# The states in three groups, batch 0's x packed by two engines, and a retimed slot table

## The chip, the core and the metric

The kernel runs on one core of a Trainium2 chip. Time is the device time of one execution in microseconds (us), a median over runs. A profile is one execution, taken by the hardware profiler; its span runs from the first to the last instruction of the program.

## What is computed

Cross attention between tokens x and a small state, both ways, and then a feed-forward layer with a snake activation on the concatenated result:

```python
# x: (8, 8, 512, 64), state: (8, 8, 32, 64); B, H, S, D = x.shape, Ns = 32
scores = scale * np.matmul(x, state.transpose(0, 1, 3, 2))
a = softmax(scores)
xread = np.matmul(a, state)                     # 512 tokens a batch
scores2 = scale * np.matmul(state, x.transpose(0, 1, 3, 2))
sread = np.matmul(softmax(scores2), x)          # 32 tokens a batch
t = np.concatenate([xread, sread], axis=2)      # 8 batches of 544 tokens, 512 wide
h = t @ w_in                                    # 512 x 2048
s = np.sin(alpha * h)
out = (h + s * s / alpha) @ w_out               # 2048 x 512
```

## The kernel before

**Tiles and slots.** The feed-forward part runs over nine tiles t: tiles 0 to 7 are the 512 read tokens of one batch each, tile 8 the 256 state tokens of all batches. A tile has 16 slots f, one for each 128 of the 2048 hidden columns. The order of each engine's instructions is that of the Python program (a manual schedule), and each engine works off its own queue in order.

In a slot, `mm1` makes a 128 x 512 block of h in a bank of the pool `psH` (four banks) on TensorE, two matmuls; ScalarE takes its sine (line 405); the square goes to VectorE (DVE, line 417) where the slot is listed in the table `SQ`, else to GpSimd (POOL, line 410); and two slots later DVE's `snake` (line 420) makes gT = s2/alpha + h and frees the bank. A tile's second product, `mm2` (line 429), is 64 matmuls of 216 ns each for four blocks of 128 tokens; the tables `TWO0`, `TWO1` and `TWO` say how many of them follow in each slot of tile 0, 1 and the later ones. When a block is done ScalarE copies it out (line 435) and SP stores it.

**Attention.** mm1 for tiles 0 to 7 does not multiply xread by w_in: `m_step` first makes M = state times w_in for each batch (16 or 8 groups of small matmuls a call, line 373, four slices `fs` of 512 columns, two halves g each), cast out of PSUM by ScalarE (line 383) or DVE (line 385) as the table 'MA' says; mm1 then multiplies M by the transposed attention weights AT. For one batch the steps are: load x (POOL, cast to bf16), `pack` (DVE), transposed x (`T` by TensorE in batches 0 and 1, `T_dma` by a transposing DMA from SP later), `S` (scores), `X` (exp on ScalarE, with a load of the table of functions before and after), `Rs` (sums, DVE), `N` (product A, on POOL, or on DVE where `ND` lists it), AT (`AT_` or `AT_dma`), and for the state tokens `W`, `Cs` and `xs`.

`BATCH` gives for each of these steps the slot, counted from the start of the batch's preceding tile (M and W: from its own tile), at which it is put into the program; batches from 3 on share the last entry. `pe` steps come after the mm1 of their slot, `post` steps at the slot's end.

**The front.** Before tile 0 the program loads all states (512 KB) and batch 0's x on SP. A copy `held` on POOL waits for the states, so that the loads of w_in ("i"), w_out ("o") and x ("x") that POOL issues behind it, in the order of `LOADS`, don't compete with them; the first `LATER` of them come at once, the others after batch 0's first product A. `prep_state` doubles all states (DVE and ScalarE), transposes them on TensorE in 16 pieces and copies them to `stT` (ScalarE, line 218). `warm_up(n)` issues n matmuls without a use. The pool `psX` (tag "px") has two banks, shared by T, S, AT_, W and the M step; `psO` has two, for mm2 and the M step.

Of the kernel before, what the change touches and what calls it, by code (L numbers as in the profile page):

```python
# [12 lines left out]
BF16 = mybir.dt.bfloat16  # L13
FP32 = mybir.dt.float32
U32 = mybir.dt.uint32
# [7 lines left out]
BATCH = {0: {'M': (-24, 1, 6, 7), 'MA': ((1, 0), (1, 1), (1, 1), (1, 1))},  # L23
 1: {'P': (1, 1),
# [4 lines left out]
     'N': (11, 9),  # L29
     'A': 14,  # L30
     'M': (-6, 1, 3, 10),
     'MA': ((1, 1), (1, 1), (1, 1), (1, 1)),
     'W': (5, 5)},
 2: {'L': -16,
     'P': (1, 3),
     'T': 5,
     'S': (6, 6),
     'X': (6, 6),
     'R': (6, 9),
     'N': (8, 10),  # L40
     'A': 12,
     'M': (-3, 1, 5, 7),
     'MA': ((0, 1), (1, 1), (1, 1), (1, 1)),
     'W': (-1, 0)},
 3: {'L': -17,
     'P': (-13, -11),
     'T': -8,
     'S': (0, 2),
     'X': (2, 2),
     'R': (5, 8),  # L50
     'N': (9, 12),
     'A': 14,
     'M': (-4, -3, 4, 4),
     'MA': ((0, 1), (1, 1), (0, 1), (1, 0)),
     'W': (-2, -2)}}

SQ = {0: (0, 1, 2, 4, 5, 8, 9, 11, 14, 15),
 1: (1, 2, 3, 5, 6, 7, 8, 11, 14),
 2: (3, 5, 6, 13, 15),
 7: (0, 1, 2, 4, 7, 8, 12),  # L60
 8: (0, 5, 7, 8, 12, 14)}
ND = {1: (), 2: (), 3: (1,)}

SLICES = {0: ((0,), (1,), (2,), (3,)), 1: ((0,), (1,), (2,), (3,)), 2: ((0, 1), (2, 3)), 3: ((0, 1), (2, 3))}
XS0 = 0

TWO0 = (0, 0, 0, 1, 2, 0, 2, 0, 2, 0, 0, 6, 1, 1, 6, 1)
TWO1 = (2, 3, 5, 1, 3, 0, 5, 2, 3, 2, 3, 5, 1, 6, 1, 0)
TWO = (1, 2, 6, 3, 10, 5, 3, 3, 4, 3, 5, 0, 5, 4, 4, 6)
WARM = (7, 1, 2, 2, 0, 1, 2)  # L70
LATER = 6

LOADS = ('i0', 'i1', 'x1', 'o0', 'i2', 'i3', 'o1', 'o2', 'o3')
# [3 lines left out]
def kernel(  # L77
# [9 lines left out]
    nc = tc.nc  # L87

    B, H, S, D = x.shape
    Ns = state.shape[2]  # L90
# [36 lines left out]
    st_nat = const.tile([P, 16, D], FP32, name="st_nat")  # L127
    nc.sync.dma_start(
        st_nat[:], state.rearrange("b h (jh jl) d -> (b h jh) jl d", jl=16)
    )  # L130
# [25 lines left out]
    nc.gpsimd.tensor_copy(held[:], st_nat[:, 0, 0:1])  # L156
# [5 lines left out]
    def load(what, k):  # L162
        k = int(k)
        if what == "x":
            load_x(k, 1)
        elif what == "i":
            cols = slice(k * FW, (k + 1) * FW)
            nc.gpsimd.dma_start(w_in_sb[:, :, cols], w_in_v[:, :, cols])  # L168
        else:
            fts = slice(k * 4, (k + 1) * 4)  # L170
            nc.gpsimd.dma_start(w_out_sb[:, fts, :], w_out_v[:, fts, :])

    for w in LOADS[:LATER]:
        load(*w)
# [7 lines left out]
    stT = const.tile([P, B * G, P], BF16, name="stT")  # L182
    nc.vector.memset(stT[:].bitcast(U32), 0)
# [15 lines left out]
    def prep_state():  # L199
        st2 = const.tile([P, 16, 2, D], BF16, name="st2")  # L200
        for half, copy in ((0, nc.vector.tensor_copy), (1, nc.scalar.copy)):
            js = slice(half * 8, (half + 1) * 8)
            copy(st2[:, js], st_nat[:, js].unsqueeze(2).to_broadcast([P, 8, 2, D]))
        for half in range(2):
            tp = psH.tile([P, 8, P], BF16, name="st_ps", tag="h")
            for k in range(8):
                nc.tensor.transpose(
                    tp[:, k, :],
                    st2[:, half * 8 + k].rearrange("p r d -> p (r d)"),
                    ident[:],  # L210
                )
            for r in range(2):
                rows = slice(r * D, (r + 1) * D)
                src = tp[rows].rearrange("d k (e r2 jh) -> d e r2 jh k", r2=2, jh=2)
                dst = stT[rows].rearrange(
                    "d bg (h2 r2 jh hf k) -> d (bg h2) r2 jh hf k", h2=2, r2=2, jh=2, hf=2
                )
                nc.scalar.copy(dst[:, :, r, :, half, :], src[:, :, r])
# [7 lines left out]
    class Att:  # L226
# [13 lines left out]
        def pack(a, g, parts=2):  # L240
            hs = slice(g * H // parts, (g + 1) * H // parts)
            nc.vector.tensor_copy(  # L242
                a.xp[:, :, hs, :],
                xnat_l[a.b][:, hs, :].rearrange("p h (i d) -> p i h d", i=C),
            )

# [27 lines left out]
        def S(a, g):  # L274
            sp = psX.tile([P, C, P], FP32, name="s_ps", tag="px")
            for i in range(C):
                for k in range(2):
                    cols = slice(k * 2 * Ns, (k + 1) * 2 * Ns)
                    nc.tensor.matmul(  # L279
                        sp[:, i, cols],  # L280
                        a.xT[:, i, 2 * g + k, :],
                        stT[:, a.b * G + g, cols],
                        start=True, stop=True,
                    )
            a.sp[g] = sp
# [71 lines left out]
    def m_step(b, slices, on_act):  # L357
# [8 lines left out]
        for fs in slices:  # L366
            for h in range(2):
                for g in range(G):
                    for r in range(2):
# [5 lines left out]
                            stT[rows, b * G + g, c0:c0 + Ns],  # L375
# [93 lines left out]
    prep_state()  # L469
# [4 lines left out]
    a.pack(0)  # L474
    a.pack(1)
# [28 lines left out]
    def add(d, s, fn, *args):  # L504
        d.setdefault(s, []).append((fn, args))
# [7 lines left out]

    for b in range(B):
        p = BATCH[min(b, 3)]
# [3 lines left out]
        if b:  # L519
# [10 lines left out]
            for g in range(G):  # L530
# [3 lines left out]
                eng = nc.vector if g in ND[min(b, 3)] else nc.gpsimd  # L534
# [80 lines left out]
```

## Time and profile before

| | us |
|---|---|
| median of 5 runs (lowest, highest) | 231.41 (230.69, 231.78) |
| the profiled execution | 230.69 |
| its span | 228.9 |
| busy: TensorE (PE), DVE, ScalarE (ACT), POOL | 212.5, 170.8, 164.6, 111.5 |
| states land, x of batch 0 lands (two halves) | 4.68; 6.19 and 7.58 |
| w_in slices land | 11.1, 13.6, 22.5, 25.1 |
| x of batches 1, 2 and 3 lands | 16.4, 35.4, 38.7 |
| first mm1; first sine of tiles 1 and 2 | 13.96; 34.2, 55.9 |

Times in the lower rows are counted from the start of the span. PE is TensorE's matmuls, PEld its weight loads, which lie beside them. Matmul ends are modelled, so a hole on TensorE is read from the starts: one start to the next, less the usual pitch of that form.

### The profile page before, as it was taken

How to read it: one execution, taken by the hardware profiler on the slowest of the kernel's cores; microseconds unless marked ns; L12 is line 12 of the kernel's file. 1: busy time of each engine (PE TensorE's matmuls, PEld its weight loads, DVE VectorE, ACT ScalarE, POOL GpSimd, SP SyncE). 2: the span in 40 equal slices, each digit the busy share in tenths (PEclk: the TensorE clock that was granted, in tenths of full speed). 3: DMA queues.
4: the chain of work that ended last, by engine and by line, in shares of the span. 5: the costliest groups of instructions: out<-in, count | busy, mean ns of one | idle time of the engine just before them, and what ended most of it. 6: DMA issues, size and time to landing. Idle time of an engine off the chain costs nothing.

```text
span 228.9 us, 4186 instructions
## 1 busy us (share of the span) xinstructions
PE 212.5 (93%) x1508; PEld 103.5 (45%) x1536; DVE 170.8 (75%) x309; ACT 164.6 (72%) x266; POOL 111.5 (49%) x120
## 2 busy tenths in 40 slices
PE   6987799799989999999999999999997999999993
PEld 2634243444434544454444444454443444556552
DVE  3699999998498969795988788877876796544500
ACT  4689979988996699667967796769783766444420
POOL 3871581265629651975168625843481135632210
PEclk9999999999999999999999999999999999999998
DMA  6999999823716381659063805220208101111112
GB/s 210 194 196 206 206 186 168 179 72 92 92 49 139 95 136 46 139 84 146 17 169 88 130 17 163 76 86 0 92 37 105 42 38 57 50 47 46 49 46 92
DMA packets 36661, 23.35 MB, mean 102 GB/s; under 512 B 19728, under 2 KB 32288, under 8 KB 36640
## 3 DMA queue, kind: packets, MB, share of 16 engines
q0 software_dynamic: 11504, 7.87, 24.4%
q1 hardware_dynamic: 24864, 14.95, 23.9%
q10 hardware_dynamic: 272, 0.27, 0.4%
q8 instruction: 12, 0.20, 0.3%
q14 instruction: 9, 0.07, 0.1%
HBM read 17.31 MB, written 8.91 MB: 115 GB/s over the span
## 4 chain that ended last, share of the span: by engine, by line
PE 73%; DMA 14%; ACT 6%; issue 2%; POOL 2%; DVE 1%; SPq 0%; ACTq 0%
PE o_ps L429 42%; PE h_ps L393 20%; DMA w_in_sb<-in_moe_w_in_dram 7%; DMA AT<-A 4%; PE h_ps L399 3%; PE m_ps L373 3%; ACT s L405 2%; DMA xT<-xp 2%; DMA st_nat<-in_state_dram 2%; ACT M L383 2%; PE o_ps L454 2%; PE s_ps L279 2%; POOL w_in_sb L168 1%; PE w_ps L324 1%; ACT o_sb L435 1%
## 5 line engine op out<-in xcount | busy, mean ns | idle before, releaser
L410 POOL TENSOR_TENSOR s<-s 128x512 bf16<-128x512 bf16 (+1 forms) x87 | 87.5, 1016 | 97.7 <-ACT s L405 78.7
L429 PE MATMUL o_ps<-w_out_sb,gT 128*128 128x512 bf16 x510 | 131.5, 379 | 2.2 <-issue 1.9
L405 ACT ACTIVATE s<-h_ps,alpha_sb 128x512 bf16<-128x512 f32 (+1 forms) x144 | 94.3, 670 | 44.1 <-PE h_ps L393 29.2
L420 DVE SCALAR_TENSOR_TENSOR gT<-s,inva_sb,h_ps 128x512 bf16<-128x512 bf16 (+1 forms) x144 | 99.7, 708 | 23.4 <-POOL s L410 22.1
L393 PE MATMUL h_ps<-AT,M 128*128 128x512 bf16 x247 | 73.1, 379 | 2.7 <-DMA AT<-A 1.8
L429 PEld LDWEIGHTS <-gT 128*128 128x128 bf16 x528 | 49.5, 98 | 57.3 <-issue 5.2
L393 PEld LDWEIGHTS <-M 128*128 128x128 bf16 x256 | 24.5, 98 | 32.2 <-DMA AT<-A 2.8
L417 DVE TENSOR_TENSOR s<-s 128x512 bf16<-128x512 bf16 (+1 forms) x57 | 24.6, 437 | 5.3 <-ACT s L405 4.4
L383 ACT CAST M<-m_ps 128x512 bf16<-128x512 f32 x48 | 25.4, 601 | 0.6 <-PE m_ps L373 0.5
L435 ACT COPY o_sb<-o_ps 128x512 f32<-128x512 f32 x33 | 19.5, 595 | 7.6 <-PE o_ps L429 7.3
L385 DVE CAST M<-m_ps 128x512 bf16<-128x512 f32 x16 | 10.6, 689 | 9.2 <-PE m_ps L373 9.2
L373 PE MATMUL m_ps<-w_in_sb,stT 64*32 64x512 bf16 x256 | 11.3, 383 | 1.7 <-DMA w_in_sb<-in_moe_w_in_dram 1.1
L292 DVE TENSOR_REDUCE R<-E 128x16 f32<-128x512 bf16 x16 | 10.8, 677 | 0.5 <-ACT E L288 0.5
L300 POOL TENSOR_TENSOR A<-E,rR 128x512 bf16<-128x512 bf16 x8 | 8.4, 1048 | 5.4 <-DVE rR L293 5.4
L288 ACT ACTIVATE E<-s_ps 128x512 bf16<-128x512 f32 x16 | 8.8, 595 | 1.2 <-PE s_ps L279 1.1
L399 PE MATMUL h_ps<-xs_all,w_in_sb 128*128 128x256 bf16 x64 | 9.6, 273 | 0.1
L288 ACT ACT_TABLE_LOAD x7 | 9.0, 1283 | 0.1
L405 ACT ACT_TABLE_LOAD x7 | 9.0, 1283 | 0.1
L279 PE MATMUL s_ps<-stT,xT 128*128 128x64 bf16 x128 | 6.2, 193 | 2.4 <-DMA xT<-xp 1.5
L399 PEld LDWEIGHTS <-w_in_sb 128*128 128x128 bf16 x64 | 6.3, 98 | 4.1
L242 DVE COPY xp<-xnat 128x1024 bf16<-128x1024 bf16 x14 | 5.6, 408 | 3.4 <-DMA xnat<-in_x_dram 3.3
L373 PEld LDWEIGHTS <-stT 64*32 64x32 bf16 x256 | 3.1, 89 | 11.0 <-issue 8.0
(51 smaller groups left out, 98.8 us busy)
## 6 DMA issues: line engine op xcount, KB each, us to landing
out_dram<-o_sb SPq DMA_DIRECT2D x32, 256.0 KB, 2.3
xnat<-in_x_dram POOLq DMA_DIRECT2D x7, 512.0 KB, 6.2
w_in_sb<-in_moe_w_in_dram POOLq DMA_DIRECT2D x4, 512.0 KB, 10.5
w_out_sb<-in_moe_w_out_dram POOLq DMA_DIRECT2D x4, 512.0 KB, 15.6
x_first<-in_x_dram SPq DMA_DIRECT2D x2, 512.0 KB, 5.4
st_nat<-in_state_dram SPq DMA_DIRECT2D x1, 512.0 KB, 3.9
out_dram<-o_sb SPq DMA_DIRECT2D x1, 128.0 KB, 2.4
out_dram<-o_sb ACTq DMA_DIRECT2D x1, 128.0 KB, 2.7
```

What stands on the lines that cost most here:

```text
L288: nc.scalar.activation(a.E[:, g], a.sp[g][:], ACT.Exp, scale=scale)
L292: nc.vector.reduce_sum(a.R[:, g], E8, axis=AX.X)
L373: nc.tensor.matmul(mp[fs, g][o0:o0 + Ns, :], stT[rows, b * G + g, c0:c0 + Ns], w_in_sb[rows, 2 * g + h, fs * FW:(fs + 1) * FW], start=True ...
L383: nc.scalar.copy(dst, mp[fs, g][:])
L393: nc.tensor.matmul(hp[:, :n], Ms[t][:, g, f * P:(f + 1) * P], atts[t].AT[:, g, :], start=(g == 0), stop=(g == G - 1),)
L399: nc.tensor.matmul(hp[:, :n], w_in_sb[:, q, f * P:(f + 1) * P], xs_all[:, q].rearrange("p h k b l -> p (h k b l)"), start=(q == 0), stop=( ...
L405: nc.scalar.activation(s[:, :n], hp[:, :n], ACT.Sin, scale=alpha_sb[:, f:f + 1])
L410: nc.gpsimd.tensor_tensor(s2[:, :n], s[:, :n], s[:, :n], ALU.mult)
L417: nc.vector.tensor_tensor(s2[:, :n], s[:, :n], s[:, :n], ALU.mult)
L420: nc.vector.scalar_tensor_tensor(gT[t][:, f, :n], s2[:, :n], inva_sb[:, f:f + 1], hp[:, :n], ALU.mult, ALU.add)
L429: nc.tensor.matmul(op[:], gT[t][:, ft, st * P:(st + 1) * P], w_out_sb[:, ft, :], start=(ft == 0), stop=(ft == FT - 1),)
L435: nc.scalar.copy(o_sb[:], op[:])
```

## The change

- The states are loaded in three groups of batches, (0), (1 to 4) and (5 to 7), each partition with 128 numbers a batch. Batch 0's load is first on SP, in fp32. Group 1 is second in POOL's list of loads ("s1", cast to bf16), group 2 is issued at slot 15 of tile 1 ("s2").
- `prep_state` becomes `double_state(k)`, on DVE, and `prep_state(k)`, on TensorE and ScalarE, one for each group: 2, 8 and 6 transposes. Group 0 is done at the front in a bank of psH; group 1 is doubled at slot 0 of tile 0 and transposed at slot 2; group 2 is doubled at slot 9 of tile 2 and transposed at slot 12, both in psX.
- Batch 0's x is packed in four quarters, alternately by DVE and ScalarE (`pack_first`).
- Batch 3 gets an entry of its own in `BATCH` and `ND`; batches from 4 on share the last one. The entries, `SQ`, the three mm2 tables and the warm-ups are set anew. In the later tiles this means: squares on DVE in 7 slots instead of 5; of a batch's eight M casts, ScalarE has 3 instead of 5; both products A on POOL at slots 10 and 11; AT_dma at slot 13 instead of 14; W and Cs at slot 13 instead of 14.

The tables:

```diff
-BATCH = {0: {'M': (-24, 1, 6, 7), 'MA': ((1, 0), (1, 1), (1, 1), (1, 1))},
+BATCH = {0: {'M': (-17, 1, 6, 8), 'MA': ((1, 0), (0, 1), (1, 0), (1, 1))},
- 1: {'P': (1, 1), 'T': (3, 3), 'S': (3, 3), 'X': (3, 3), 'R': (3, 7), 'N': (11, 9), 'A': 14,
-     'M': (-6, 1, 3, 10), 'MA': ((1, 1), (1, 1), (1, 1), (1, 1)), 'W': (5, 5)},
+ 1: {'P': (1, 2), 'T': (3, 3), 'S': (3, 3), 'X': (3, 3), 'R': (3, 7), 'N': (10, 9), 'A': 14,
+     'M': (-6, 0, 2, 10), 'MA': ((1, 1), (1, 0), (1, 1), (1, 1)), 'W': (4, 4)},
- 2: {'L': -16, 'P': (1, 3), 'T': 5, 'S': (6, 6), 'X': (6, 6), 'R': (6, 9), 'N': (8, 10), 'A': 12,
-     'M': (-3, 1, 5, 7), 'MA': ((0, 1), (1, 1), (1, 1), (1, 1)), 'W': (-1, 0)},
+ 2: {'L': -14, 'P': (1, 1), 'T': 2, 'S': (6, 6), 'X': (6, 6), 'R': (7, 10), 'N': (7, 10), 'A': 11,
+     'M': (-2, 1, 6, 10), 'MA': ((0, 1), (1, 1), (1, 1), (1, 1)), 'W': (-1, 0)},
- 3: {'L': -17, 'P': (-13, -11), 'T': -8, 'S': (0, 2), 'X': (2, 2), 'R': (5, 8), 'N': (9, 12), 'A': 14,
-     'M': (-4, -3, 4, 4), 'MA': ((0, 1), (1, 1), (0, 1), (1, 0)), 'W': (-2, -2)}}
+ 3: {'L': -10, 'P': (-5, -4), 'T': -4, 'S': (2, 2), 'X': (2, 2), 'R': (2, 6), 'N': (2, 9), 'A': 10,
+     'M': (-6, 3, 4, 7), 'MA': ((0, 1), (1, 1), (0, 1), (1, 0)), 'W': (-3, -3)},
+ 4: {'L': -18, 'P': (-13, -11), 'T': -5, 'S': (1, 2), 'X': (2, 2), 'R': (4, 10), 'N': (10, 11), 'A': 13,
+     'M': (-4, -2, 4, 4), 'MA': ((1, 0), (0, 0), (0, 1), (1, 0)), 'W': (-3, -3)}}
-SQ = {0: (0, 1, 2, 4, 5, 8, 9, 11, 14, 15), 1: (1, 2, 3, 5, 6, 7, 8, 11, 14),
- 2: (3, 5, 6, 13, 15), 7: (0, 1, 2, 4, 7, 8, 12), 8: (0, 5, 7, 8, 12, 14)}
-ND = {1: (), 2: (), 3: (1,)}
+SQ = {0: (2, 4, 8, 9, 11), 1: (1, 5, 6, 7, 8, 12, 13),
+ 2: (0, 3, 5, 6, 11, 13, 15), 7: (1, 2, 4, 5, 6, 7, 9, 10, 13, 14), 8: (1, 2, 7, 9, 10, 11, 14, 15)}
+ND = {1: (), 2: (), 3: (), 4: ()}
+GROUPS = ((0,), (1, 2, 3, 4), (5, 6, 7))
+ST = (0, 2, 31, 41, 44)
-TWO0 = (0, 0, 0, 1, 2, 0, 2, 0, 2, 0, 0, 6, 1, 1, 6, 1)
-TWO1 = (2, 3, 5, 1, 3, 0, 5, 2, 3, 2, 3, 5, 1, 6, 1, 0)
-TWO = (1, 2, 6, 3, 10, 5, 3, 3, 4, 3, 5, 0, 5, 4, 4, 6)
-WARM = (7, 1, 2, 2, 0, 1, 2)
-LATER = 6
+TWO0 = (0, 0, 0, 0, 0, 1, 1, 3, 1, 4, 1, 3, 2, 0, 1, 4)
+TWO1 = (1, 4, 4, 1, 0, 4, 1, 3, 1, 6, 6, 0, 4, 7, 1, 0)
+TWO = (2, 1, 6, 3, 10, 2, 5, 1, 7, 2, 4, 1, 8, 2, 4, 6)
+WARM = (8, 4, 3, 2, 0, 0, 0)
+LATER = 7
-LOADS = ('i0', 'i1', 'x1', 'o0', 'i2', 'i3', 'o1', 'o2', 'o3')
+LOADS = ('i0', 's1', 'i1', 'x1', 'o0', 'i2', 'i3', 'o1', 'o2', 'o3')
```

The code:

```diff
-    st_nat = const.tile([P, 16, D], FP32, name="st_nat")
-    nc.sync.dma_start(
-        st_nat[:], state.rearrange("b h (jh jl) d -> (b h jh) jl d", jl=16)
-    )
+    st_v = state.rearrange("b h (jh jl) d -> (h jh) b (jl d)", jl=2)
+    st_nat = const.tile([P, 2 * D], FP32, name="st_nat")
+    nc.sync.dma_start(st_nat[:], st_v[:, 0])
...
+        elif what == "s":
+            bs = GROUPS[k]
+            st_b[k] = const.tile([P, len(bs), 2 * D], BF16, name="st_b%d" % k)
+            nc.gpsimd.dma_start(st_b[k][:], st_v[:, bs[0]:bs[-1] + 1])
...
+    def double_state(k):
+        n = len(GROUPS[k])
+        src = st_nat if k == 0 else st_b[k]
...
+        nc.vector.tensor_copy(
+            st2[k][:],
+            src.rearrange("p (bj d) -> p bj d", d=D).unsqueeze(2)
+            .to_broadcast([P, 2 * n, 2, D]),
+        )
+    def prep_state(k, pool, tag):
+        n = len(GROUPS[k])
+        tp = pool.tile([P, 2, n, P], BF16, name="st_ps", tag=tag)
+        for b in range(n):
+            for jl in range(2):
+                nc.tensor.transpose(
+                    tp[:, jl, b, :],
+                    st2[k][:, 2 * b + jl].rearrange("p r d -> p (r d)"),
+                    ident[:],
+                )
+        for r in range(2):
...
+            nc.scalar.copy(dst[:, r], src[:, r])
...
+        def pack_first(a):
+            for q in range(Q):
+                copy = nc.scalar.copy if q % 2 else nc.vector.tensor_copy
+                hs = slice(2 * q, 2 * q + 2)
+                copy(
+                    a.xp[:, :, hs, :],
+                    xnat_l[a.b][:, hs, :].rearrange("p h (i d) -> p i h d", i=C),
+                )
...
+    add(post, ST[0], double_state, 1)
+    add(pe, ST[1], prep_state, 1, psX, "px")
+    add(post, ST[2], load, "s", 2)
+    add(post, ST[3], double_state, 2)
+    add(pe, ST[4], prep_state, 2, psX, "px")
     for b in range(B):
-        p = BATCH[min(b, 3)]
+        p = BATCH[min(b, 4)]
```

## The prediction

> **What bounds the kernel now.** I read the stage table first, then the chain of waits, then the sum of TensorE's waits. In the stage table each row is one stretch of the span: its length, then busy time of PE, PEld, DVE, ACT and POOL. The rows are tile 0 in two parts, then tiles 1 to 7, then the tail.
>
> ```profile
> core 0: us, PE busy (x) PEld busy (x) DVE busy (x) ACT busy (x) POOL busy (x), PEclk, DMA share, GB/s
> 14.00:25.60 11.60, 8.51 (x79) 3.72 (x81) 11.21 (x24) 10.92 (x18) 4.21 (x6) 1.00 1.28 205
> 25.60:34.20 8.60, 8.55 (x52) 3.94 (x54) 8.25 (x15) 7.07 (x12) 7.01 (x7) 1.00 1.25 195
> 34.20:55.90 21.70, 19.90 (x175) 9.04 (x176) 20.25 (x39) 20.12 (x35) 8.22 (x8) 1.00 0.59 123
> 55.90:80.40 24.50, 23.49 (x177) 11.12 (x178) 20.02 (x36) 19.51 (x33) 15.49 (x15) 1.00 0.47 99
> 80.40:104.50 24.10, 23.23 (x170) 10.66 (x170) 20.00 (x36) 18.55 (x30) 13.56 (x13) 1.00 0.58 100
> 104.50:128.00 23.50, 23.13 (x172) 10.87 (x171) 18.78 (x34) 18.52 (x30) 13.57 (x13) 1.00 0.45 100
> ...
> 151.50:176.40 24.90, 23.24 (x162) 10.58 (x162) 18.72 (x33) 18.57 (x31) 12.69 (x12) 1.00 0.29 63
> ```
>
> Two regimes. In tiles 0 and 1 DVE is busy 39.7 of 41.9 us (ACT 38.1), so DVE sets the pace. From tile 2 on TensorE does: the undisturbed tile (104.5 to 128) is 23.5 us, and every tile above that has a hole. The chain of waits (start, length, what) names the holes:
>
> ```profile
> 0.74 3.94 DMA st_nat<-in_state_dram
> 4.73 0.71 POOL held L156
> ...
> 9.63 15.49 DMA w_in_sb<-in_moe_w_in_dram
> ...
> 38.92 4.12 DMA xT<-xp
> 43.09 0.64 PE s_ps L279 x16
> ...
> 97.15 1.40 ACT M L383 x3
> 98.57 0.64 ACT o_sb L435
> 99.72 4.04 DMA AT<-A
> ...
> 170.84 4.79 DMA AT<-A
> ```
>
> And TensorE's waits by cause (total, times, longest):
>
> ```profile
> PE h_ps L393 <- DMA AT<-A: 1.8, 2, 1.3
> PE s_ps L279 <- DMA xT<-xp: 1.5, 1, 1.5
> PE m_ps L373 <- DMA w_in_sb<-in_moe_w_in_dram: 1.1, 1, 1.1
> PE m_ps L373 <- ACT o_sb L435: 0.6, 1, 0.6
> ```
>
> The holes, from one TensorE start to the next less the usual pitch: 1.23 us at 25.2 (slice 3 of w_in), 1.70 at 43.1 (xT of batch 2), 0.76 at 64.1 (the M step of tile 2 waits for ScalarE to free an output bank), 0.67 at 103.8 and 1.45 at 175.7 (AT landing late for tiles 4 and 7). The usual AT lands in 2.73 us; the two late ones took 4.04 and 4.79, because a 16 KB instruction fetch (the page's queue q8, 12 packets) fell among their 256-byte packets, some of which then took 1.2 to 2.2 us.
>
> **Front.** The state of batch 0 alone is 64 KB, 128 packets of 512 B. State packets of 4 KB held the 16 engines for about 1.6 us; the new ones, at the 40 to 47 ns that the small x_first packets take, for 0.4. So it lands near 2.9 instead of 4.68, x_first 1.3 earlier (4.9 and 6.3), and the held copy (0.71) lets POOL issue the weights at 3.6 instead of 5.44: 1.8 earlier. POOL then issues seven loads instead of six (0.85 each), done at 9.6, just ahead of its first product A at about 10.
>
> TensorE: the eighth warm-up ends at 1.26 + 8 x 0.426 = 4.7; two transposes replace sixteen (1.9 us busy at L207), and two ScalarE copies of an eighth of the work, about 0.25 each, replace four of 0.58. Pack by two engines: before, two casts of 0.69 and 1.00 on DVE; after, two halves on DVE (0.35) and two on ScalarE (about 0.55), done by 6.9 instead of 8.6. Then T, S, exp, sums, A and AT as before. First mm1 about 12.4 instead of 13.96. Here a rule bears: the Trainium skill, "TensorE: Matmul & The Clock Gate", "What's actually happening", has TensorE at full rate after about 3.4 us of sustained work. The trace shows 426 ns warm-ups, then a 1.3 us hole, and the 56 ns transposes only at 7.5, 6.2 us after the first warm-up. By the rule the four new warm-ups run at 216 ns and end at 6.0, before the pack; by the row they may run at 426 and end at 6.9, which holds T(0) 0.6 us. I take the rule, as the hole is gone; 0.6 goes into the range.
>
> **The price of group 1's load.** It goes second in POOL's queue: 512 packets written with 256 B, and everything behind it is later by its time. The skill, "DMA: Bandwidth & Descriptors", "Specifications", wants 512 B or more per transfer and names a read-modify-write below; that speaks against this change. The rows: 512 packets of 1 KB (a w_in slice) took 2.5 us between landings, 1024 packets of 512 B (x of batch 1) 2.75. The line through both gives 0.8 us for 512 packets of 256 B; as dear as 512 B ones they cost 1.4; doubled by the rule, 2.8. I take 1.1. Against the 1.8 us earlier start, w_in slices 1 to 3 and the x of batches 1 and 2 land 0.7 earlier (x of batch 2: 35.4 to 34.7); by the rule, 1.0 later.
>
> **Tiles 0 and 1.** DVE's sum for tile 0, in pitches of the trace: five squares fewer (-5 x 0.42), two casts of M more (+2 x 0.65), one doubling of group 1 more (+0.69; bound 0.3 to 1.0, nearest row the pack and st rows): nothing, -0.1. So DVE is earlier by its earlier start, 1.8 us (inva_sb done at 12.8, not 14.8), less what it newly waits for: prep_state(1) at slot 2 shares the two "px" banks with the M step at slot 1, whose first half DVE now casts only after the doubling and xs, so TensorE stands until about 15.7; and ScalarE does two copies of 1.2 together before the exp of batch 1, so its sin of slot 4 begins 0.4 earlier only (21.7, not 22.1). ScalarE loses two M casts in tile 0 (-1.2), which pays those copies. The w_in slice 3 stall shrinks: the slice is used one slot later. POOL takes 11 squares instead of 6: four in a row, slots 12 to 15, at 1.04 each end near 34, so snake of slot 15 comes at 34.7. Both packs of batch 2 stand at slot 1 of tile 1 and wait for x of batch 2 (34.7): both done near 35.9, where before one was done at 36.3. The xT transfer starts at 36, lands at 40.1, and S, at about slot 6's old time, no longer waits 1.7 us. But the DVE work behind it stays: 16 snakes, 7 squares instead of 9 (-0.84), one M cast more (+0.65). So tile 2 starts earlier by 0.8 to 1.6; I take **-1.2**. Bounds: 0 (x of batch 2 late by the rule, and DVE waits) and -2.5 (the whole earlier start plus the xT hole).
>
> **Tile 2.** Its M step moves from slot 5 to 6, two more mm2 and one mm1 behind the output copy: the 0.76 hole goes. The second prep_state is new: six transposes (0.34), a fill of 0.1 to 0.3, and possibly a wait of 0.3 for a "px" bank freed by the M step of slot 10: +0.45. ScalarE's 0.95 and DVE's 0.5 lie beside TensorE, which has 4 us more to do in this tile than either. Together **-0.3**.
>
> **Tiles 3 to 6.** TensorE's work is the same (64 mm2, 16 mm1, 32 M matmul groups a tile). ScalarE drops two M casts per batch, DVE takes them (+1.3) with two squares more (+0.84) and gives the second A to POOL (-0.65): +1.5, so about 20.3 of 23.5. At slot 12 three DVE casts now stand before the snake of slot 10. Walked from the trace's pitches that snake ends 1.2 us before mm1 of slot 14 needs its bank, and the snake of slot 12, behind xs at slot 13, 0.9 us before the next tile's first mm1. So nothing is lost, with 0.9 to spare. AT: A is finished by POOL after slot 11; the store ahead of it on SP waits for the output copy, which now has one cast before it on ScalarE, not three: AT is issued about 4.5 us before mm1 needs it instead of 3.7. A delayed AT (4.0) still fits; one of 4.8 would cost 0.3. So 0.67 and 1.45 go: **-2.1**.
>
> **Sum.** -1.2 - 0.3 - 2.1 = -3.6 on a span of 228.9: 225.3; with the 1.8 around it (230.69 - 228.9) 227.1. The profiled execution was the lowest of five, 0.7 below the median of 231.41, so against the median **227.8**.
>
> **Rivals.**
> (a) Front gain swallowed: x of batch 2 and slice 3 come late by the packet price, DVE waits, and tile 1 ends as before; AT gain stays for one tile only. -0.3 - 0.7 - 0 = 230.4. For it: the queue is full from 7 to 35 us (205 GB/s rows). Against: 1.8 us earlier start. Chance 0.17; half of it lies within the noise.
> (b) Front gain kept whole: -2.5 - 0.3 - 2.1 = 226.5. For it: the xT hole vanishes and ScalarE and DVE are within 5% of each other. Against: DVE's sum. Chance 0.13.
> (c) Slower: DVE becomes the bound in tiles 3 to 6, at the three casts of slot 12. It decides once DVE is later than my walk by 0.9 us; each us beyond costs four times. If casts and squares take their recorded 0.69 and 0.45 instead of the pitch, and snakes 0.74, DVE has some 2.2 us more in a tile, of which 1.3 count: +5.2 - 3.6 = 233. For it: 23.5 less 20.3 leaves little for waits on POOL's squares, which now also stand behind two A products. Against: before, DVE shows idle time in each such tile. Chance 0.17.
>
> The forecast has 0.53. Below 0.3% (0.7 us) this kernel's measurement can't tell a change. Faster: 0.53 + 0.13 + 0.07; same 0.08; slower 0.19. The range 226.0 to 232.0 holds (a), most of (b), and the mild half of (c).
>
> **What would show it.** Right: the held copy near 3, first mm1 near 12.4, x of batch 2 landing before 35.4, no wait of S for xT, no hole near tile 2's first M step, no wait for AT at tiles 4 and 7, tiles 3 to 6 at 23.5. Wrong: mm1 waiting for gT (DVE) in slots 13 to 15, packs waiting beyond 36, or AT waits at other tiles.

## The result, and the profile after

| | before | after |
|---|---|---|
| median, us (runs) | 231.45 (50) | 229.81 (29) |
| ratio after to before, 95% interval | | 0.993 (0.9917 to 0.9944) |
| the profiled execution, its span | 230.69, 228.9 | 229.37, 227.5 |

The kernel became 0.7% faster: 1.64 us by the medians, where 3.6 had been forecast. The direction was right and the time lies in the range, but less than half of the gain came. The starts of the tiles (first sine of each) say where it was lost:

| tile | 0 | 1 | 2 | 3 | 4 | 5 | 6 | 7 | 8 | end of span |
|---|---|---|---|---|---|---|---|---|---|---|
| before, us | 15.0 | 34.2 | 55.9 | 80.4 | 104.5 | 128.0 | 151.5 | 176.4 | 197.8 | 228.9 |
| after, us | 13.9 | 33.4 | 55.5 | 80.8 | 104.4 | 128.0 | 151.5 | 175.1 | 196.5 | 227.5 |
| after less before | -1.1 | -0.8 | -0.4 | +0.4 | -0.1 | 0.0 | 0.0 | -1.3 | -1.3 | -1.4 |

Tile 0 begins 1.1 us earlier, of which 0.4 is left when tile 2 begins. Tile 2 is 0.8 longer, so tile 3 begins 0.4 late. Only the two tiles whose AT had come late, 3 and 6, are shorter, and they make the whole result. (The loss of AT's wait shows as a shorter tile 3 and a shorter tile 6, since tiles 4 and 7 are those that waited for it.)

The stage table of the changed kernel, with the columns and the same kind of rows as before (tile 0 in two parts, tiles 1, 2, 3, 4 and 6):

```profile
core 0: us, PE busy (x) PEld busy (x) DVE busy (x) ACT busy (x) POOL busy (x), PEclk, DMA share, GB/s
13.00:24.50 11.50, 8.23 (x76) 3.88 (x77) 11.03 (x23) 10.66 (x18) 6.51 (x8) 1.00 1.26 201
24.50:33.40 8.90, 8.85 (x65) 3.74 (x64) 8.71 (x15) 7.37 (x13) 7.90 (x8) 1.00 1.21 189
33.40:55.50 22.10, 21.14 (x177) 9.41 (x173) 20.55 (x37) 19.58 (x33) 13.29 (x14) 1.00 0.58 120
55.50:80.80 25.30, 24.21 (x174) 11.27 (x177) 22.75 (x37) 20.55 (x34) 13.97 (x14) 1.00 0.47 98
80.80:104.40 23.60, 23.19 (x167) 10.76 (x169) 20.35 (x38) 17.65 (x28) 12.30 (x12) 1.00 0.55 102
104.40:128.00 23.60, 23.21 (x166) 10.77 (x168) 20.37 (x38) 17.66 (x28) 12.28 (x12) 1.00 0.48 101
151.50:175.10 23.60, 23.20 (x167) 10.73 (x169) 20.01 (x36) 17.80 (x29) 11.21 (x11) 1.00 0.18 57
```

Tiles 3 to 6 are as forecast: DVE 20.4 of 23.6 us (forecast 20.3), and all of one length. Tile 2 stands out: DVE is 22.75 us busy, 2.7 more than before, with one instruction more (37 for 36). A busy time that grows so much with so little work is a lengthened instruction, and the groups of DVE's instructions in tile 2 name it (the last of each row: count, then busy us and mean ns, then the idle time before; first the kernel before, then the one after):

```profile
L417 DVE TENSOR_TENSOR s<-s 128x512 bf16<-128x512 bf16 x5 | 2.5, 526 | 0.0
```

```profile
L460 DVE TENSOR_TENSOR s<-s 128x512 bf16<-128x512 bf16 x6 | 5.4, 918 | 0.0
...
L276 DVE COPY xp<-xnat 128x1024 bf16<-128x1024 bf16 x2 | 1.4, 704 | 0.0
```

The squares take 918 ns on average instead of 526, and the packs 704 where the same copy had taken 395. TensorE's waits, over the whole span (total, times, longest), no longer name AT, xT, w_in or o_sb (ScalarE's copy of an output bank). First one row of the kernel before, then rows of the changed one:

```profile
PE h_ps L393 <- DVE gT L420: 0.5, 1, 0.5
```

```profile
PE h_ps L436 <- DVE gT L463: 2.2, 4, 1.0
...
PE st_ps L239 <- ACT M L426: 0.6, 1, 0.6
```

All four waits that the prediction quoted are gone, 5.0 us in sum. In their place stand mm1's waits for DVE's snake (2.2 us; before, 0.5), the longest of them in tile 0 (0.95 at 21.9), and one for the cast of M ahead of the new transposes of the states. The waits for packs in tile 0 come to 0.7 us, 0.6 before. So waits of 5.0 us went, and the span is 1.4 us shorter.

The changed kernel's DVE and POOL in the first 5 us of tile 2 (timeline: start, length, what; the bracket is idle time of that engine and who ended it). The first row is POOL's issue of the load of state group 2:

```profile
56.70 0.80 POOL L183 DMA_DIRECT2D st_b<-in_state_dram  x1
57.17 0.75 DVE L463 SCALAR_TENSOR_TENSOR gT<-s,inva_sb,h_ps 128x512 bf16<-128x512 bf16 x1
...
57.52 2.04 POOL L453 TENSOR_TENSOR s<-s 128x512 bf16<-128x512 bf16 x2
57.83 2.02 DVE L460 TENSOR_TENSOR s<-s 128x512 bf16<-128x512 bf16 x1
...
59.89 0.75 DVE L463 SCALAR_TENSOR_TENSOR gT<-s,inva_sb,h_ps 128x512 bf16<-128x512 bf16 x1
...
60.69 0.59 PE L436 MATMUL h_ps<-AT,M 128*128 128x512 bf16 x2 [0.71 <-DVE gT L463]
```

The square of slot 0, which the new `SQ` puts on DVE, is issued 0.31 us after POOL's first of two squares in a row, and is over 0.29 us after POOL's second (57.52 + 2.04 = 59.56; 57.83 + 2.02 = 59.85). Alone it takes 0.42. The snake behind it comes late (experiment 1 tells by how much), and mm1 stands. Over all DVE squares and packs of both traces the picture is the same: of the squares that do not meet a POOL tensor operation none is late (47 of 47 in each kernel), and of the 26 squares and packs that start while one runs, 24 end 0.28 to 0.29 us after POOL; the other two started just before its end and took 0.42 us, as alone. Added up over squares, packs and products (duration less that of the same form alone), this costs DVE 2.1 us before and 5.7 after. That POOL's second square went first as well is the exception (experiment 4 returns to it): a pack at 49.6 met two POOL operations in a row too and came between them.

### The profile page after: what moved, and what is told of

Read it like the earlier page. It is cut to its first block, busy times and chain, and to the rows that moved or that the text cites. A ratio compares the mean times of both kernels' runs of the same rounds, so it can differ in the third digit from the quotient of the medians.

```text
span 227.5 us, 4176 instructions
## 1 busy us (share of the span) xinstructions
PE 213.9 (94%) x1510; PEld 103.1 (45%) x1538; DVE 178.4 (78%) x327; ACT 160.2 (70%) x258; POOL 108.7 (48%) x119
## 4 chain that ended last, share of the span: by engine, by line
PE 68%; DVE 11%; ACT 6%; DMA 5%; issue 5%; POOL 3%; SPq 0%; POOLq 0%; ACTq 0%
PE o_ps L472 40%; PE h_ps L436 17%; DVE gT L463 4%; PE h_ps L442 3%; DMA xnat<-in_x_dram 3%; PE m_ps L416 3%; DMA x_first<-in_x_dram 2%; ACT s L448 2%; POOL s L453 2%; DVE s L460 2%; PE o_ps L497 2%; DVE R L335 1%; PE w_ps L367 1%; ACT M L426 1%; DVE xp L276 1%
## 5 line engine op out<-in xcount | busy, mean ns | idle before, releaser
L448 ACT ACTIVATE s<-h_ps,alpha_sb 128x512 bf16<-128x512 f32 (+1 forms) x144 | 93.3, 669 | 45.3 <-PE h_ps L436 32.6
L453 POOL TENSOR_TENSOR s<-s 128x512 bf16<-128x512 bf16 (+1 forms) x79 | 78.5, 1005 | 96.2 <-ACT s L448 95.4
L463 DVE SCALAR_TENSOR_TENSOR gT<-s,inva_sb,h_ps 128x512 bf16<-128x512 bf16 (+1 forms) x144 | 99.0, 708 | 14.8 <-POOL s L453 13.9
L436 PE MATMUL h_ps<-AT,M 128*128 128x512 bf16 x247 | 74.0, 379 | 3.1 <-DVE gT L463 2.2
L460 DVE TENSOR_TENSOR s<-s 128x512 bf16<-128x512 bf16 (+1 forms) x65 | 29.3, 466 | 6.0 <-ACT s L448 5.7
L478 ACT COPY o_sb<-o_ps 128x512 f32<-128x512 f32 x33 | 19.5, 591 | 8.9 <-PE o_ps L472 8.6
L428 DVE CAST M<-m_ps 128x512 bf16<-128x512 f32 x27 | 17.4, 685 | 6.4 <-PE m_ps L416 6.3
L426 ACT CAST M<-m_ps 128x512 bf16<-128x512 f32 x37 | 19.9, 593 | 0.5 <-PE m_ps L416 0.5
L276 DVE COPY xp<-xnat 128x1024 bf16<-128x1024 bf16 x14 | 7.4, 533 | 5.0 <-DMA xnat<-in_x_dram 5.0
L387 DVE RECIPROCAL rC<-w_ps 128x128 f32<-128x128 f32 x8 | 7.6, 951 | 0.4 <-PE w_ps L378 0.4
## 6 DMA issues: line engine op xcount, KB each, us to landing
st_b<-in_state_dram POOLq DMA_DIRECT2D x1, 128.0 KB, 6.1
out_dram<-o_sb SPq DMA_DIRECT2D x1, 128.0 KB, 2.4
out_dram<-o_sb ACTq DMA_DIRECT2D x1, 128.0 KB, 2.7
```

Of the source, the lines that this page charges most:

```text
L426: nc.scalar.copy(dst, mp[fs, g][:])
L428: nc.vector.tensor_copy(dst, mp[fs, g][:])
L436: nc.tensor.matmul(hp[:, :n], Ms[t][:, g, f * P:(f + 1) * P], atts[t].AT[:, g, :], start=(g == 0), stop=(g == G - 1),)
L448: nc.scalar.activation(s[:, :n], hp[:, :n], ACT.Sin, scale=alpha_sb[:, f:f + 1])
L453: nc.gpsimd.tensor_tensor(s2[:, :n], s[:, :n], s[:, :n], ALU.mult)
L460: nc.vector.tensor_tensor(s2[:, :n], s[:, :n], s[:, :n], ALU.mult)
```

## Experiments

Two theories stood at the start. **Port:** DVE's squares and packs can't run beside POOL's, the new tables make them meet more often, and tile 2 pays for it. **Rival:** the new, early sums and products of batch 3 (slots 2 to 9 of tile 2 instead of 5 to 12) crowd DVE's first slots. For the front: that the gain is swallowed by the new work in tile 0 and by the weights.

**1. The square of tile 2's slot 0 back on POOL**, in the changed kernel, nothing else.

```diff
+ 22: (3, 5, 6, 11, 13, 15),
-        return t if t < 2 or t >= B - 1 else 2
+        return t if t < 2 or t >= B - 1 else 22 if t == 2 else 2
```

> The changed kernel with one square, slot 0 of tile 2, moved from DVE to POOL. Port theory (a DVE instruction with two SBUF inputs, or a pack, that meets a running POOL product waits until POOL is done): the 2.02 us square at 57.8 and the 0.88 us TensorE hole at 60.7 go; tile 2 (25.3 us) shrinks by 0.6 to 0.9, the span by 0.4 to 0.9 to about 226.8. Rival (batch 3's sums at slot 2 hold DVE while they wait for the exp): hole and span stay within 0.2.

228.98 us, ratio to before 0.9892 (0.9859 to 0.9924); span 226.8. This interval overlaps that of the changed kernel, so the gain is read from tile 2: 24.35 us, against 25.33 or 25.34 in the three profiles whose tile 2 is that of the changed kernel (its own, experiments 9 and 10). The same stretch of the timeline:

```profile
57.70 3.03 POOL L454 TENSOR_TENSOR s<-s 128x512 bf16<-128x512 bf16 x3
58.78 0.75 DVE L464 SCALAR_TENSOR_TENSOR gT<-s,inva_sb,h_ps 128x512 bf16<-128x512 bf16 x1 [0.69 <-POOL s L454]
...
59.98 0.59 PE L437 MATMUL h_ps<-AT,M 128*128 128x512 bf16 x2
```

POOL does three squares in a row, and the snake, which now waits for POOL openly, still starts 1.1 us earlier than it did behind DVE's own square. mm1 follows with no hole. A square handed to the slower engine made tile 2 1.0 us shorter: the port theory holds for this hole.

**2. The sums of batch 3 later**, in the changed kernel.

```diff
-     'R': (2, 6), 'N': (2, 9),
+     'R': (5, 8), 'N': (5, 9),
```

> The changed kernel with batch 3's sums and product A back at slots 5 and 8 (product at 5 and 9) instead of 2 and 6. Rival theory (the early sums hold DVE): the hole at 60.7 goes and the span falls by 0.6 to 0.9. Port theory: the 2.02 us square and the hole at 60.7 stay, since nothing ahead of them has moved; the span changes by less than 0.4 either way.

229.0 us, 0.9898 (0.9865 to 0.9932); span 227.0; tile 2 24.9. The hole at 60.7 (0.88 us) and the long square stay:

```profile
57.79 2.02 DVE L460 TENSOR_TENSOR s<-s 128x512 bf16<-128x512 bf16 x1
```

So the rival is not the cause of that hole. Tile 2 still gained 0.4, as the pack and the square that had met POOL near 62 to 64 no longer do (DVE is late by 5.1 us in all instead of 5.7).

**3. Experiments 1 and 2 together.**

> The changed kernel with both single edits of the runs before: slot 0's square of tile 2 on POOL, and batch 3's sums later. Port theory: the 2.0 us square is gone, and the pack at 62 and the square at 63.6 no longer meet product A: DVE's delay by meetings falls from 5.6 to about 2.8 us; tile 2 at 24.0 to 24.3, span 226.3 to 226.8. If the two are not additive: 226.8 to 227.2.

228.2 us, 0.9846 (0.9826 to 0.9866); span 226.5. It beats both kernels. Its tile 2:

```profile
55.60:79.60 24.00, 23.68 (x174) 11.21 (x177) 20.50 (x36) 20.34 (x35) 14.95 (x15) 1.00 0.50 103
```

DVE falls from 22.75 to 20.50 us in this tile, and in the whole kernel it is late by 3.5 us. Tile 2 is 1.3 us shorter than in the changed kernel, nearly the sum of the two edits alone (1.0 and 0.4).

**4. The tables alone**: the states, the front and the loads of before, with the slot tables of after.

```diff
-BATCH, SQ, ND, TWO0, TWO1, TWO of the kernel before
+BATCH, SQ, ND, TWO0, TWO1, TWO of the changed kernel
```

> The kernel before with all states loaded and transposed at the front, and the slot tables, square, product and cast tables of the change. If the gain at tiles 4 and 7 is the tables' own: tiles 3 and 6 at 23.5 to 23.8, no AT hole over 0.3; and the 2 us square in tile 2, if squares and POOL's products meet there again, costs 0.5 to 0.9. Span 227.2 to 228.5; below the change's 227.5 if the states' groups bring nothing.

231.22 us, 0.9962 (0.9937 to 0.9987); span 230.4. No wait for AT is left, so that gain belongs to the tables. But DVE is late by 7.2 us in all (squares of 1.28 and 1.23 us at 89.9 and 137.7, in tiles 3 and 5, which are 24.3 us long; tiles 4 and 6 are 23.4). Tile 2 is only 24.0 us, as in experiment 3, though slot 0's square is on DVE and the sums are early:

```profile
60.29 2.22 POOL L421 TENSOR_TENSOR s<-s 128x512 bf16<-128x512 bf16 x2 [0.54 <-ACT s L416]
...
60.84 0.77 DVE L428 TENSOR_TENSOR s<-s 128x512 bf16<-128x512 bf16 x1
```

The square meets POOL here too, but comes between POOL's two, takes 0.77 us, and no hole follows. Counted from the tile's start, DVE's square begins at 2.36 us in both kernels, POOL's two at 1.81 here and at 2.05 in the changed kernel. There the issue of group 2's load (0.80 us at 56.70) stands ahead of them in POOL's queue; here there is no such load. So the new tables alone don't make the long square; with that load ahead of POOL's squares they do (no run moved the load alone). (TensorE's granted clock was half from 19.3 to 22.7 us in the profiled execution, so tile 0 of it isn't read.) The median hides something: six of the eleven runs show a mean granted clock of 0.989 to 0.993 and took 231.2 to 232.5 us, the five at 0.996 or more took 229.9 to 230.4. The median of these five, 230.16, is 1.4 us below that of the kernel before in the same session (231.58). Where TensorE keeps its clock, the tables alone give nearly the whole gain of the change. Whether the lost clock is this kernel's own was not tried; in the profiled execution TensorE had been busy 1.57 of the 3.45 us ahead of it, while the changed kernel, busy 2.37 us from 16.0 to 19.4, kept its clock.

**5. The states and the front alone**: the code, loads and warm-ups of after, with the tables of before; group 2's transposes two slots earlier.

```diff
-BATCH, SQ, ND, TWO0, TWO1, TWO of the changed kernel; ST = (0, 2, 31, 41, 44)
+BATCH, SQ, ND, TWO0, TWO1, TWO of the kernel before; ST = (0, 2, 31, 41, 42)
```

> The state groups, the new front and batch 0's two-engine pack, with every table of the kernel before; group 2 is transposed at slot 10 of tile 2 to stay clear of the M step at slot 12. If the front's gain is kept: first sine near 13.5, tile 1 starts 1.0 to 1.5 earlier than before (34.2), span 227 to 228. If it is not (new work in tile 0's first slots and the weight queue eat it): tile 1 starts within 0.5 of before, AT holes as before, TensorE's six transposes on top, span 228.5 to 229.5.

232.6 us, 1.0042 (1.0027 to 1.0057); span 231.5. Alone, this half makes the kernel slower. Tile 0 begins at 13.1, 1.9 earlier than before, and tile 1 at 34.6, 0.4 later (here too the clock was half, from 19.5 to 22.9, so the size of that isn't read). Tile 2 is 26.6 us: an M step waits for DVE's snake, a hole of 1.58 us at 66.1, behind a pack that met POOL (1.01 us at 64.4). So nearly all of the change's gain is that of the tables. Under the old tables the new states and front cost time; with the new ones tile 0 begins 1.1 us earlier, but tile 2 is 1.3 us longer than in experiment 4.

**6. Only the M casts of the later batches, in the kernel before.** The prediction had said that AT is issued earlier because fewer casts stand ahead of the output copy on ScalarE.

```diff
-      'MA': ((0, 1), (1, 1), (0, 1), (1, 0)),
+      'MA': ((1, 0), (0, 0), (0, 1), (1, 0)),
```

> The kernel before, with one edit: of a later batch's eight M casts ScalarE has 3 and DVE 5, as in the change; AT stays at slot 14. Theory (AT was late because its issue on SP stands behind a store that waits for ScalarE's casts): AT of batches 4 to 7 is issued 0.8 to 1.2 us earlier against mm1, the 0.67 hole at tile 4 goes, the 1.45 one at tile 7 shrinks to 0.5 or less; span 227.2 to 227.9. Rival (AT was late by the instruction fetch alone): AT is still collided with and issued as late; span 228.5 or more. If DVE's three casts at slot 12 cost what the slower case said, tiles 3 to 6 grow by over 0.5 each.

233.73 us, 1.008 (1.0045 to 1.0114); span 232.1. The chain of waits still has both late AT:

```profile
101.05 4.56 DMA AT<-A
174.02 4.92 DMA AT<-A
```

AT is issued 4.4 and 4.1 us ahead of the time at which tiles 4 and 7 would begin without its hole (106.4 - 0.9 - 101.05, 179.7 - 1.6 - 174.02); before, that is 4.1 both times, in the changed kernel 5.1 at tile 4 (4.4, counted to the first mm1, which comes some 0.7 ahead of the sine). And DVE's shifted order now meets POOL in tiles 2 to 6 (eight squares of 1.10 to 1.14 us; 6.9 us lost in all), which may be most of the loss. So the casts alone do not bring AT forward; which of the table's other moves does (AT at slot 13, A on POOL) was not separated.

**7. The instruction fetch moved**, in the kernel before: four warm-ups replaced by 40 short ones, so that TensorE's program is some 72 records longer ahead of tile 0.

```diff
-    warm_up(WARM[0])
+    warm_up(3)
+    wp = psO.tile([P, S], FP32, name="o_ps", tag="o")
+    for _ in range(40):
+        nc.tensor.matmul(wp[:, 0:64], warm[:, 0:P], warm[:, 0:64], start=True, stop=True)
```

> The kernel before, with 4 of the 7 first warm-ups replaced by 40 of 64 columns, which shifts every later place of TensorE's instruction stream by 72 and nothing else. Fetch theory (AT of batches 4 and 7 took 4.0 and 4.8 us because a 16 KB fetch of TensorE's instructions fell into them): the fetch comes some 2 us earlier against AT, all six AT transfers take 2.7 to 2.9, the holes of 0.67 and 1.45 go, span 226.7 to 227.3. Rival (a fixed property of these two transfers, or contention by x loads): they stay at 4 us and more, span 228.5 to 229.

233.26 us, 1.0054 (1.0021 to 1.0087); span 229.9, of an execution (231.68) that was the fourth fastest of twelve. The chain of waits:

```profile
76.68 4.93 DMA AT<-A
...
148.66 4.49 DMA AT<-A
```

The two AT that had been late now land in 2.75 and 2.73 us, and two others are late, those of batch 3 and batch 6. The fetch of 16 KB itself starts at 78.62 and 150.55 instead of 83.52 and 153.49, within those transfers. Over all fourteen profiles, the 28 AT transfers during which such a fetch begins took 4.04 to 5.08 us, and the other 56 took 2.71 to 2.75. That it is the fetch which delays AT is shown; the gain expected in time failed, as other transfers were hit.

**8. An early xT, in the kernel before**, to see whether the 1.70 us hole at 43.1 was on the path. A first try at slot 2 left the transfer behind SP's two stores of that slot; a second one put it at slot 1.

```diff
- 2: 'P': (1, 3), 'T': 5,
+ 2: 'P': (1, 1), 'T': 2,     (first try)
+ 2: 'P': (1, 1), 'T': 1,     (second try)
```

> The kernel before, with batch 2's packs and its transposing DMA at slots 1 and 2 of tile 1, as in the change, not 1, 3 and 5. As predicted (the 1.70 hole at 43.1 is on the path): hole gone, tile 2 starts 0.8 to 1.7 earlier, span 227.2 to 228.1. Cover theory (ScalarE's own chain from the sine of slot 6 through two table loads and the exp, 4.4 us to the next sine, runs over the hole): hole gone, but the sine of slot 7 and the start of tile 2 move by less than 0.3.

231.38 us, 1.0 (0.998 to 1.0021). The hole of 1.71 stayed: it tells nothing.

> The kernel before with both packs of batch 2 at slot 1 of tile 1 and the transposing transfer of its xT issued at slot 1 too, ahead of the stores of slot 2 (the earlier try left it behind them). Theory (ScalarE's own chain, sine of slot 6, table load, two exp, table load, sine of slot 7, 4.4 us long, covers the hole): the 1.70 us hole of TensorE at 43.1 shrinks below 0.6, and tile 2 still starts at 55.5 to 56.1; ratio to before 0.997 to 1.003. Rival (the hole was on the path, as the prediction had it): tile 2 starts at 54.2 to 54.8, span about 227.5, ratio about 0.993.

231.06 us, 0.9976 (0.9954 to 0.9998). The transfer is out at 37.94 instead of 38.92, against a tile 1 that begins 1.3 us later (35.5; its profiled execution lost that in tile 0), so it is 2.2 us earlier in the tile. S waits 0.4 us less, since its second half now waits for DVE's xs, and ScalarE does not begin earlier. First ScalarE of the kernel before, then of this one:

```profile
41.59 0.69 ACT L405 ACTIVATE s<-h_ps,alpha_sb 128x512 bf16<-128x512 f32 x1 [0.38 <-PE h_ps L393]
42.30 1.28 ACT L288 ACT_TABLE_LOAD   x1
43.59 1.09 ACT L288 ACTIVATE E<-s_ps 128x512 bf16<-128x512 f32 x2
44.70 1.28 ACT L405 ACT_TABLE_LOAD   x1
45.99 1.27 ACT L405 ACTIVATE s<-h_ps,alpha_sb 128x512 bf16<-128x512 f32 x2
```

```profile
42.84 0.69 ACT L405 ACTIVATE s<-h_ps,alpha_sb 128x512 bf16<-128x512 f32 x1 [0.37 <-PE h_ps L393]
...
47.23 1.27 ACT L405 ACTIVATE s<-h_ps,alpha_sb 128x512 bf16<-128x512 f32 x2
```

From the sine of slot 6 to that of slot 7 it is 4.40 us in both (45.99 - 41.59, 47.23 - 42.84), and 4.40 in the changed kernel, where S does not wait for xT at all. So in this stretch ScalarE does not feel the hole. But TensorE does: it works on without a hole behind it, and at slot 12 ScalarE waits for TensorE, less in this run. First the kernel before, then this one:

```profile
51.12 1.40 ACT L405 ACTIVATE s<-h_ps,alpha_sb 128x512 bf16<-128x512 f32 x2 [0.59 <-PE h_ps L393]
```

```profile
52.02 1.40 ACT L405 ACTIVATE s<-h_ps,alpha_sb 128x512 bf16<-128x512 f32 x2 [0.32 <-PE h_ps L393]
```

The hole shrank by 0.43 us (1.70 to 1.27; below 0.6 had been expected), and tile 1 by 0.34, to 21.28; in all five profiles with the old tables in tile 1 and the full hole it is 21.62 to 21.64. So the theory that the chain covers the hole fails in part. The hole was worth something at its end, if not 1.7 us: behind it ScalarE waits for TensorE by 0.59 and 0.25 us in the rest of tile 1, about 0.8 in all. The measured gain of 0.24% is at the edge of what can be told.

**9. A later front, in the changed kernel**: four matmuls of warm-up directly ahead of the first mm1.

```diff
     nc.vector.reciprocal(inva_sb[:], inva_sb[:])
+    warm_up(4)
```

> The changed kernel with four matmuls of warm-up (0.86 us together) put directly ahead of the first mm1, so that tile 0 begins nearly as late as before the change. Theory (what tile 0 gains at its front it loses in its own first slots and to the weights, so the front is worth little): first sine at about 14.7, tile 1 starts at 33.3 to 33.7 all the same, ratio to before 0.991 to 0.995. Rival (each us of the front reaches the end): tile 1 starts at 34.2 to 34.3, span 228.3, ratio to before 0.996 to 0.998.

230.11 us, 0.993 (0.9897 to 0.9964), the changed kernel's own ratio; span 228.3. TensorE did part of the warm-ups while it would have waited for AT, so the first mm1 came 0.61 us later (13.50 for 12.89), the first sine 0.3 (14.2), and tile 1 0.3 (33.7). In this execution the 0.3 was passed on, as the rival has it, and another 0.5 came in tile 3, at whose end mm1 waited 0.37 us for a snake; by the median no loss can be told. It does not decide.

**10. The second pack of batch 1 ahead of the snake of slot 0**, in the changed kernel, and the same on top of experiment 3.

```diff
- 1: {'P': (1, 2),
+ 1: {'P': (1, 1),
```

> The changed kernel with the second pack of batch 1 one slot earlier, so that on DVE it stands ahead of the snake of slot 0 instead of behind it. Theory (the first slots of tile 0 have more work than room, and the weights come later anyway): the 0.54 and 0.57 us holes at the T and S groups of batch 1 shrink, but tile 1 starts at 33.1 to 33.6, less than 0.3 us earlier; ratio to before 0.991 to 0.995. Rival (the pack behind the snake is what loses the front gain): tile 1 starts at 32.5 to 32.9, span about 226.8, ratio about 0.989.

229.24 us, 0.9901 (0.9866 to 0.9937), span 227.5. The waits move, they do not go: of TensorE's waits between 14 and 24 us, that for the packs falls from 0.7 to 0.5 us and that for xT grows from 0.4 to 0.8.

> The three edits together on the changed kernel: the square of slot 0 of tile 2 on POOL, the sums of batch 3 three slots later, and the second pack of batch 1 ahead of the snake of slot 0. Theory (the pack's place is worth under 0.3 us): 227.9 to 228.4, ratio to before 0.983 to 0.987. Rival (the pack's place brings the front gain back): 227.4 to 227.8, ratio about 0.981.

228.24 us, 0.9855 (0.9822 to 0.9888); span 226.9: as experiment 3 without it. The pack's place is worth nothing that can be told.

What caps the front can be read from all these profiles, whose programs are nearly the same up to tile 1 (in experiments 1, 2 and 3 exactly so):

| | exp. 1 | both edits and pack | exp. 2 | pack first | exp. 3 | changed | late front |
|---|---|---|---|---|---|---|---|
| first sine of tile 0 | 13.2 | 13.3 | 13.4 | 13.5 | 13.7 | 13.9 | 14.2 |
| first sine of tile 1 | 33.6 | 33.9 | 33.4 | 33.2 | 33.5 | 33.4 | 33.7 |

Whether tile 0 begins at 13.2 or 13.9, tile 1 begins near 33.5. In experiments 1 to 3 and the combined kernel TensorE stands in tile 0 for the second slice of w_out; here is experiment 3's:

```profile
26.46 0.59 PE L473 MATMUL o_ps<-w_out_sb,gT 128*128 128x512 bf16 x2 [0.18 <-DMA w_out_sb<-in_moe_w_out_dram]
```

The hole is 0.35 us there, 0.47 in experiment 2, 0.87 in experiment 1 and 0.93 in the combined kernel; the slice landed at 26.3 to 26.8. The kernel with the pack first began tile 0 at 13.5 without this hole, as its slice landed at 26.14. So in four of the five kernels that began ahead of 13.9 the weights (the DMA moved 205 and 201 GB/s in the first part of tile 0, before and after) took some of the lead; a fixed limit isn't shown.

## Why the prediction was right in sign and wrong in size

**Front: nearly right.** The state landed at 2.85 (forecast 2.9), POOL issued from 3.16 (3.6), the first mm1 came at 12.89 (12.4; x of batch 0 came 0.6 to 0.7 later than forecast, 5.59 and 6.94). Group 1's load took 0.73 us between landings, not 1.1. The line through the two rows of the trace (0.8) describes these 512 packets of 256 B; the doubled price, 2.8, does not. That factor was the prediction's own estimate: the Trainium skill ("DMA: Bandwidth & Descriptors", "Specifications") names a read-modify-write below 512 B, but no factor. The x of batch 2 landed at 33.72, a full us earlier than forecast. The four warm-ups ended at 6.53, between the two forecasts (the granted clock was full from 5.82), and held nothing: T(0) began at 6.37, as the first quarter that ScalarE packed ended at 6.35.

**Tiles 0 and 1: the term of -1.2 was wrong; it came to -0.4.** Two steps failed. First, tile 1 was priced by DVE's work and the hole of xT alone, and what the new tables do in its last slots was put at nothing. The hole went, as forecast, and some of it came through: counted from the tile's start, the sine of slot 14 comes at 18.98 us instead of 19.98. But the next sine comes 2.49 us behind it instead of 1.06, and tile 1 ends 0.4 longer than before, at 22.05. The M step of batch 2 moved one slot later, so its three casts and an output copy now stand on ScalarE between these two sines; before, they filled the time in which ScalarE waits for TensorE, which now passes idle (1.26 us, while TensorE does seven mm2). First the kernel before, then the changed one:

```profile
52.41 1.55 ACT L383 CAST M<-m_ps 128x512 bf16<-128x512 f32 x3
54.22 0.69 ACT L405 ACTIVATE s<-h_ps,alpha_sb 128x512 bf16<-128x512 f32 x1 [0.25 <-PE h_ps L393]
...
55.27 1.28 ACT L405 ACTIVATE s<-h_ps,alpha_sb 128x512 bf16<-128x512 f32 x2
```

```profile
52.40 0.69 ACT L448 ACTIVATE s<-h_ps,alpha_sb 128x512 bf16<-128x512 f32 x1 [1.26 <-remote]
52.99 1.55 ACT L426 CAST M<-m_ps 128x512 bf16<-128x512 f32 x3
54.41 0.62 ACT L478 COPY o_sb<-o_ps 128x512 f32<-128x512 f32 x1
54.89 1.31 ACT L448 ACTIVATE s<-h_ps,alpha_sb 128x512 bf16<-128x512 f32 x2
```

This is read from the traces: no run moved the M step alone, and how much of the 1.0 us of lead is the hole's was not separated. Second, the front's earlier start was held to reach tile 2 less what DVE newly waits for; but tile 0 gives back 0.3 of 1.1 by itself (mm1 waits 0.95 us for a snake at 21.9, 0.51 before), and in four of five kernels that began earlier still the second slice of w_out took some, which the prediction did not follow (it had followed slice 3 of w_in and the x).

**Tile 2: the term of -0.3 was wrong; it came to +0.8.** The 0.76 hole went, as said. The step that failed is that DVE's work would "lie beside TensorE", at the price that its forms have alone. `SQ` of this tile takes slot 0 onto DVE while POOL squares, and the early sums bring DVE's packs beside POOL's product. Squares were priced at 0.42 each, a price that holds only where POOL is idle; this one took 2.02, and mm1 waited 0.7 us for the snake behind it. And of group 2's states only the doubling, the transposes and the copies were priced: the issue of their load on POOL was put at nothing, yet without it the same tables have no such square (experiment 4). The kernel before shows the effect already (a square of 0.95 us at 64.0, while POOL worked): the longest of the group, not its mean, would have told. The Trainium skill states the rule ("SBUF — State Buffer", section "SBUF: two separate sides"): DVE, with two SBUF inputs or in a two-port mode, and GpSimd take one pair of ports in turn, and the one that starts second is fully blocked for the length of the other's instruction. The trace agrees: the DVE instruction ends 0.28 us after POOL's. By the rule a square that meets one POOL square of 1.04 us takes up to 1.3, an estimate from these two numbers; that POOL's second square went first too, though DVE's had started before it, is in the trace (2.02) and not in the rule. Experiment 1 took that one meeting away, and tile 2 was 1.0 us shorter.

**Tiles 3 to 6: right in mechanism, near in size.** -2.1 was forecast and -1.8 came (94.25 us for the four tiles, 96.02 before). AT was issued 4.4 us before it was needed (forecast 4.5). The fetches hit the same two transfers again (4.31 and 4.57 us), and only 0.2 us of hole is left, at tile 7. DVE had room, as walked: no wait for a snake at slots 13 to 15. The reason given for the earlier issue, fewer casts ahead of the output copy, is not borne out: the casts alone moved the issue by 0.3 us at most and cost 0.8% (experiment 6).

**The rivals.** The one that ends at 230.4, "front gain swallowed", is the nearest in time, and right in that the front's gain did not get through; but its reason, late transfers by the price of small packets, was wrong: the transfers came early. DVE did not become the bound in the later tiles, so the slower case did not come. The sum of the misses, 0.8 for tiles 0 and 1, 1.1 for tile 2 and 0.3 for the later tiles, is 2.2; the forecast span was 225.3, the measured one 227.5.

**Open:** which of the tables' moves brings AT forward; how much of tile 1's loss is the M step's place (DVE's packs at 49.6 and 51.1 also took 0.92 and 0.60 us beside POOL); and what lets POOL's second square go ahead of DVE's: with DVE's start 0.31 us behind POOL's first it did, with 0.55 it did not.

## What to carry to other kernels

Before a hole is counted as a gain, ask which other engine's chain runs through the same stretch, and where the waiting engine is next waited for; here two table loads and two exp ran beside 1.7 us of hole, and 0.43 us of it was worth 0.34 only some slots later. A gain has then to pass what the new order put behind it: 1.0 us of lead was lost again between two sines at the tile's end. When work is handed from POOL to DVE, look at what POOL runs at that moment: a DVE instruction with two SBUF inputs that starts beside it costs the rest of POOL's instruction, and moving one square of 0.42 us back to the slower engine made its tile 1.0 us shorter here. Price an instruction by the spread of its durations and not by its mean. When a change has two parts, measure each alone: here one part brought the gain.

## What the runs showed of the hardware

- A bf16 square or pack on DVE that started during a POOL tensor operation ended 0.28 to 0.29 us after it (24 of 26 in two traces). Where POOL ran two operations back to back, the outcome differed: the square at 57.8 waited for both (2.02 us for 0.42), a pack at 49.6 and in experiment 4 a square at 60.8 came between, and POOL's second operation then took 1.22 us instead of 1.04. The snakes, which read one of their inputs from PSUM, took at most 0.75 us, whether POOL ran or not.
- A fetch of 16 KB of instructions (queue q8), every 14 to 23 us, stretches the transposing transfer of AT that it meets from 2.73 to between 4.0 and 5.1 us (28 of 28, against 56 without). Four warm-up matmuls replaced by 40 short ones, far ahead, moved two fetches from 83.5 and 153.5 to 78.6 and 150.6 us, and the delay to the transfers of other batches.
- 512 packets of 256 B with a cast to bf16 took 0.73 us between landings; 512 packets of 1 KB took 2.5 us, and the line through 1 KB and 512 B packets gives 0.8.
- TensorE's granted clock fell to half for 3.4 us in the profiled executions of experiments 4 and 5, after 3.4 us in which TensorE was busy 1.57 and 1.35 us.
